# Storing output tiles of two batches with one transfer, and the order of the batches in the buffer for x

## The chip, the cores and the metric

The kernel runs on one core of a Trainium2 chip, as one launch. The metric is the device time of a launch in microseconds (us); all times below are in us unless ns is written. A launch works through five engines with instruction streams of their own: TensorE (PE in the profile, its weight loads PEld), VectorE (DVE), ScalarE (ACT), GpSimd (POOL) and SyncE (SP). SP does no arithmetic here, it issues transfers.

## What is computed

Blockwise causal attention, then a gated linear unit with a causal convolution over the sequence. Eight batches, eight heads, sequence 576, head width 64, model width 512:

```
scores = q @ k.T / 8, positions of later blocks of 64 masked
attn   = softmax(scores);  x = attn @ v        # x: 8 x 576 x 512, heads side by side
gate   = sigmoid(sum over 5 taps of conv_w[k] * x shifted by 4-k)
out    = (gate * (x @ w_val)) @ w_out          # float32, 8 x 576 x 512
```

## The kernel before

The work is cut into 32 pairs of heads, pair p being heads 2g and 2g+1 of batch b with b, g = divmod(p, 4). For each pair q and k are loaded, cast to fp16 and transposed, the scores go through the exponential on ScalarE, the product with v is normalised on VectorE (`norm`, L304) into a ring of four buffers x16, and the result is transposed into the buffer for x, `xts` (L149). The transpose goes one of two ways: through TensorE and a VectorE copy (`xtrans` L312, `evac_x` L326, words xtr and xt), or as a transposing transfer issued by SP (`xtrans_dma` L320, word xd).

`xts` holds 5 slots, each one batch of x: 128 partitions by 4 groups g by the sequence, with a few zero columns in front for the convolution. SLOT (L332) says which slot a batch takes. Eight batches share five slots, so the later ones write over earlier ones.

The second half goes by tiles. Tiles n = 0 to 7 are positions 0 to 511 of batch n. The last 64 positions of each batch are gathered: tile 8 has those of batches 0 to 3 (256 columns), tile 9 those of batches 4 to 7. ORDER (L333) gives the sequence 0, 1, 2, 3, 8, 4, 5, 6, 7, 9. `span` (L339) is the view of x that a tile reads: one slot for n below 8, and four neighbouring slots for tiles 8 and 9. For each tile there is a convolution on TensorE (`conv`, word cn), the tanh on ScalarE (`gate`, th), x @ w_val (`val`), the product of both on VectorE (`gated`, gv), and then for each block of 128 rows the product with w_out (`proj`, word o), its copy from PSUM to the output buffer `osb` by VectorE or ScalarE (`evac_out` L400, word oc) and a store (`store` L404, word st).

`osb` has NO = 5 buffers, given out in the order of TILES (L334), so an oc waits until the store five output tiles earlier has landed: (4,3) and (6,0) come after (8,0) and (4,3) in the same buffer, (5,0) after (8,1).

A block of 128 rows of tile 8 or 9 covers 64 positions of each of two batches. `store` writes these with two transfers of 64 partitions (loop at L409). Tile 8 has two blocks of 512 columns, (8,0) and (8,1). Tile 9 has (9,0) with 512 columns and its second block cut in two halves of 256 columns, (9,1) and (9,2). The last store of (9,2) is issued by ScalarE, all others of these by SP. In `xts` the batches 4 to 7 stand in falling order in slots 4 to 1, so the rows of tile 9 are those of batches 7, 6, 5, 4.

The order of all work is written out by hand: the string PLAN (L15) is a list of words that is run through from front to back, and each engine takes its own instructions in that order. The end of it, with the stores of tile 9:

```
o.7.4@3 gv.9.3 o.7.3@0 oc.7.4@A o.9.0@1 oc.7.3@D st.7.4 st.7.3 o.9.2@0 oc.9.0@A o.9.1@2 oc.9.2@D
st.9.0 oc.9.1@A st.9.2 st.9.1
```

After @ stand the PSUM banks, or the engine (A is ScalarE, D VectorE, P GpSimd). Waits between the engines, and between transfers and engines, follow from which data an instruction reads and writes. Transfers issued by SP and ScalarE share eight semaphores in rotation, and a transfer waits until the one eight before it has landed.

Of the kernel before, what the change touches and what calls it, by code (L numbers as in the profile page):

```python
# [90 lines left out]
def kernel(  # L91
# [10 lines left out]
    nc = tc.nc  # L102
# [5 lines left out]
    B, H, SEQ, D = q.shape  # L108
# [8 lines left out]
    X0 = 16  # L117
# [3 lines left out]
    def const(shape, dt, tag):  # L121
        return cpool.tile(shape, dt, tag=tag, name=tag)
# [26 lines left out]
    xts = const([128, 5, 4, X0 + SEQ + 64], fp16, "xt")  # L149
# [14 lines left out]
    def f16(i):  # L164
        return f32(i).bitcast(fp16)
# [154 lines left out]
    def xtrans_dma(p, m):  # L320
        b, g = divmod(p, 4)
        nc.sync.dma_start_transpose(
            out=xts[0:128, SLOT[b], g, X0:X0 + 640].rearrange("p (i t) -> p i t", t=128),
            in_=x16[p % NX16][0:128].rearrange("p i h d -> p (i h d)"))

    def evac_x(p, m):  # L326
        b, g = divmod(p, 4)
        nc.vector.tensor_copy(out=xts[0:128, SLOT[b], g, X0:X0 + SEQ],  # L328
                              in_=f16(bank["xtr", p])[:, 0:SEQ])


    SLOT = (0, 1, 2, 3, 4, 3, 2, 1)  # L332
    ORDER = (0, 1, 2, 3, 8, 4, 5, 6, 7, 9)  # L333
    TILES = [(n, t) for n in ORDER for t in range({7: 5, 8: 2, 9: 3}.get(n, 4))]  # L334

# [3 lines left out]
    def span(n, rows, g, back):  # L339
        if n < B:  # L340
            return xts[rows, SLOT[n], g, X0 - back:X0 - back + 512]
        return xts[rows, n - 8:n - 4, g, X0 + 512 - back:X0 + SEQ - back]

    def conv(n, *a):
        (*h, m), w = a, width(n)
        rows = [2 * h[0], 2 * h[0] + 1] if h else range(4)
        for row, b in zip(rows, m):
            bank["cn", n, row] = b
        for kk in range(5):
            for d in range(4):  # L350
                for row in rows:
                    g = (row + d) % 4
                    rs, cs = slice(32 * row, 32 * row + 32), slice(32 * g, 32 * g + 32)
                    mm(f32(bank["cn", n, row])[cs, 0:w], DG[rs, 5 * g + kk, 0:32], span(n, rs, g, 4 - kk),
                       start=(kk == 0), stop=(kk == 4))
# [20 lines left out]
    def val(n, x, m):  # L376
        bank["val", n, x] = m[0]
        for fc in range(4):
            mm(f32(m[0])[:, 0:width(n)], w_val_sb[0:128, fc, 128 * x:128 * x + 128],
               span(n, slice(0, 128), fc, 0), start=(fc == 0), stop=(fc == 3))  # L380
# [8 lines left out]
    def row(n, t):  # L389
        return min(t, {7: 3, 9: 1}.get(n, t))  # L390
# [13 lines left out]
    def store(n, t, m):  # L404
        c, o = cols(n, t), osb[0:128, TILES.index((n, t)) % NO]
        if n < B:
            (nc.scalar if t == 4 else nc.sync).dma_start(out=out[n, 128 * row(n, t):128 * row(n, t) + 128, c], in_=o[:, c])
            return
        for h in range(2):  # L409
            s = n - 8 + 2 * row(n, t) + h  # L410
            (nc.scalar if (n, t, h) == (9, 2, 1) else nc.sync).dma_start(
                out=out[s if n == 8 else 8 - s, 512:SEQ, c], in_=o[64 * h:64 * h + 64, c])

    def cols(n, t):
        z = t - {7: 3, 9: 1}.get(n, 9)
        return slice(256 * z, 256 * z + 256) if z >= 0 else slice(0, 512)
# [16 lines left out]
    def warm(m):  # L433
# [5 lines left out]
        "wv": scale_w_val, "wo": cast_w_out, "tq": trans, "Lqr": load_first, "cqr": cast_first, "tqr": trans_first, "kz": ends, "s": scores, "e": exps,  # L439
        "m": mask, "av": av, "n": norm, "xtr": xtrans, "xd": xtrans_dma, "xt": evac_x,  # L440
        "cn": conv, "th": gate, "val": val, "gv": gated, "o": proj, "oc": evac_out, "st": store,
        "cw": taps, "cT": evac_taps, "DG": diags, "w": warm, "Lcn": load_conv,
    }
# [58 lines left out]
```

## Time and profile before

| what | value |
|---|---|
| median of 3 runs | 171.03 (170.36 to 171.4) |
| time of the profiled execution | 171.92 |
| its span, first to last instruction | 170.1 |
| granted TensorE clock, mean | 0.981 |
| TensorE busy | 158.8 (93%) |
| VectorE busy | 127.8 (75%) |
| ScalarE busy | 125.7 (74%) |
| GpSimd busy | 98.8 (58%) |
| L411 stores on SP | 9, issued from 135.6 to 167.0 |
| L411 stores on ScalarE's queue | 1, issued at 164.9 |
| data written to HBM | 9.44 MB |

The profile is one execution, recorded by the hardware. Its times count from the first instruction. The page gives each engine's busy time, the chain of work that ended last, and groups of instructions by line; further views of the same trace list instructions in order of time (the timeline), transfers (the DMA view: packets, bytes, share of the 16 DMA engines, issues with the time to landing), and waits. A line of the timeline reads: start, busy time, engine and line, operation, output<-input, count, and in brackets the idle time before it with what ended it. SPq and ACTq are the instruction queues of SP and ScalarE: the issue of a transfer is shown there, not its flight. A transfer has landed when its semaphore has reached the full count.

### The profile page before, as it was taken

The numbers are of one execution on the slowest core, as the hardware profiler recorded it, in microseconds if no ns is written. First come the engines' busy times: TensorE is split into PE (matmuls) and PEld (weight loads), VectorE is DVE, ScalarE is ACT, GpSimd is POOL, SyncE is SP. The second block draws the span as 40 slices with busy tenths as digits, with TensorE's granted clock in tenths as the row PEclk, the third lists the DMA queues.
The fourth block names the chain that finished last, engine by engine and source line by source line (L and its number), as shares of the span: only waits on it lengthen the run. The fifth ranks groups of instructions, "written<-read, shape, count | busy, mean of one in ns | idle before, by whom it ended". The sixth has DMA issues, their size and how long they took to land.

```text
span 170.1 us, 7366 instructions
## 1 busy us (share of the span) xinstructions
PE 158.8 (93%) x3121; PEld 102.0 (60%) x3121; DVE 127.8 (75%) x271; ACT 125.7 (74%) x155; POOL 98.8 (58%) x190
## 2 busy tenths in 40 slices
PE   7769999999999999999989999999999999999970
PEld 2346877567675666587556766656756558454550
DVE  3884789879699989888986778766999459729540
ACT  5499999898886999789775897768787971440330
POOL 5279999996969469939760799265672362000000
PEclk9995999999999999999999999999999999999996
DMA  5999999999999605999798969993899899564554
GB/s 187 369 335 396 368 323 319 338 337 365 305 284 390 162 0 139 284 302 322 216 250 312 262 117 235 310 300 84 206 296 230 181 126 173 128 233 185 191 193 116
DMA packets 56027, 41.97 MB, mean 247 GB/s; under 512 B 46005, under 2 KB 46517, under 8 KB 55994
## 3 DMA queue, kind: packets, MB, share of 16 engines
q1 hardware_dynamic: 55770, 41.31, 85.3%
q8 instruction: 24, 0.39, 1.0%
q10 hardware_dynamic: 224, 0.20, 0.3%
q14 instruction: 9, 0.07, 0.1%
HBM read 30.42 MB, written 9.44 MB: 234 GB/s over the span
## 4 chain that ended last, share of the span: by engine, by line
PE 80%; ACT 5%; DMA 4%; DVE 3%; POOL 2%; issue 1%; SPq 1%; POOLq 0%; DVEq 0%
PE B L112 76%; ACT pt L278 5%; DMA qks<-in_q_dram 4%; PE B L315 3%; DVE x L308 1%; DVE xt L328 1%; SPq L174 1%; POOL qk L223 1%; DVE w_val L231 1%; DVE qT L239 0%; POOL v16t L220 0%; POOL v L217 0%; DVE rc L307 0%; POOL pt L286 0%; ACT osb L223 0%
## 5 line engine op out<-in xcount | busy, mean ns | idle before, releaser
L278 ACT ACTIVATE pt<-B 128x1024 f16<-128x1024 f32 x96 | 92.0, 1029 | 12.7 <-PE B L112 11.7
L223 POOL CAST qk<-qks 128x1152 f16<-128x1152 f32 (+2 forms) x31 | 41.3, 1343 | 10.4 <-DMA qks<-in_q_dram 5.5
L112 PEld LDWEIGHTS <-pt 128*128 128x128 f16 x960 | 34.2, 98 | 8.3 <-issue 1.9
L112 PE MATMUL B<-v,pt 128*128 128x65 f16 x896 | 36.4, 194 | 2.0 <-issue 1.0
L112 PE MATMUL B<-xt,w_val 128*128 128x512 f16 (+1 forms) x160 | 35.8, 359 | 0.4 <-DVE x L308 0.4
L112 PE MATMUL B<-w_out,gv 128*128 128x512 f16 (+1 forms) x152 | 36.2, 368 | 0.0
L112 PE MATMUL B<-qT,kT 32*128 32x448 f16 (+3 forms) x640 | 34.0, 292 | 2.1 <-DVE qT L239 1.1
L308 DVE TENSOR_TENSOR x<-B,rc 128x320 f16<-128x320 f32 x64 | 31.5, 492 | 2.4
L384 DVE SCALAR_TENSOR_TENSOR gv<-th,B 128x512 f16<-128x512 f32 (+1 forms) x40 | 24.5, 630 | 8.1 <-PE B L112 5.0
L372 ACT ACTIVATE th<-B 128x1024 f32<-128x1024 f32 (+1 forms) x20 | 17.7, 941 | 16.2 <-PE B L112 9.7
L112 PEld LDWEIGHTS <-kT 32*128 32x128 f16 x640 | 18.5, 93 | 16.4 <-issue 11.1
L112 PEld LDWEIGHTS <-w_val 128*128 128x128 f16 x160 | 14.0, 98 | 14.0 <-issue 2.1
L217 POOL CAST v<-vst 128x512 f16<-128x512 f32 x32 | 19.6, 618 | 4.0 <-PE B L112 1.7
L239 DVE STREAM_TRANSPOSE kT<-qk 128x576 f32<-128x576 f32 (+2 forms) x17 | 19.6, 1160 | 1.5 <-POOL qk L223 1.5
L112 PEld LDWEIGHTS <-gv 128*128 128x128 f16 x152 | 13.4, 98 | 11.0 <-issue 0.8
L239 DVE STREAM_TRANSPOSE qT<-qk 128x576 f32<-128x576 f32 (+3 forms) x18 | 19.4, 1103 | 0.4 <-POOL qk L223 0.3
L307 DVE RECIPROCAL rc<-B 128x5 f32<-128x5 f32 x64 | 11.8, 184 | 10.4 <-PE B L112 10.0
L286 POOL MEMSET pt<- 64x384 f16 x32 | 13.3, 414 | 9.8 <-ACT pt L278 8.1
L223 DVE COPY osb<-B 128x512 f32<-128x512 f32 (+1 forms) x21 | 13.7, 658 | 6.3 <-PE B L112 6.2
L285 POOL COPY pt<-pt 128x128 f16<-128x128 f16 x32 | 9.6, 301 | 13.2 <-ACT pt L278 12.8
L223 ACT COPY osb<-B 128x512 f32<-128x512 f32 (+1 forms) x17 | 9.5, 574 | 7.8 <-PE B L112 4.4
L112 PE MATMUL B<-xt,DG 32*32 32x512 f16 (+1 forms) x800 | 13.1, 356 | 0.0
(45 smaller groups left out, 112.6 us busy)
## 6 DMA issues: line engine op xcount, KB each, us to landing
qks<-in_k_dram SPq DMA_DIRECT2D x16, 576.0 KB, 6.3
qks<-in_q_dram SPq DMA_DIRECT2D x16, 576.0 KB, 6.8
vst<-in_v_dram SPq DMA_DIRECT2D x64, 128.0 KB, 5.4
out_dram<-osb SPq DMA_DIRECT2D x31, 256.0 KB, 3.1
vtst<-in_v_dram SPq DMA_DIRECT2D x8, 128.0 KB, 6.7
th<-in_moe_w_val_dram SPq DMA_DIRECT2D x2, 512.0 KB, 7.1
osb<-in_moe_w_out_dram SPq DMA_DIRECT2D x2, 512.0 KB, 5.7
out_dram<-osb SPq DMA_DIRECT2D x7, 128.0 KB, 2.4
```

The costliest lines, as they stand in the source:

```text
L112: nc.tensor.matmul(out=out, lhsT=lhsT, rhs=rhs, start=start, stop=stop, skip_group_check=True)
L217: nc.gpsimd.tensor_copy(out=v16s[p % NV][0:128, 0:4, 0:2, 0:64], in_=vst[p % NVS][0:128])
L223: (eng.copy if eng is nc.scalar else eng.tensor_copy)(out=o, in_=i)
L239: nc.vector.transpose(out=(qT, kT)[i][a % NQT][0:128].bitcast(fp32).rearrange("p c (x n) -> p c n x", n=9)[:, :, x // 2:y // 2], in_=qk16[ ...
L278: nc.scalar.activation(out=pts[(2 * a + r) % NPT][0:128, 0:2, 512 * t:512 * t + 512], in_=two(bank["s", a, t, 2 * r], bank["s", a, t, 2 * ...
L285: nc.gpsimd.tensor_copy(out=pt[0:128, 0:2, 1536:1600], in_=pt[0:128, 0:2, 0:64])
L286: nc.gpsimd.memset(pt[64:128, 0:2, 0:1536].rearrange("p h (t s) -> p h t s", t=3)[:, :, :, 0:64], 0.0)
L307: nc.vector.reciprocal(out=rc[0:128], in_=O[:, :, 64:65])
L308: nc.vector.tensor_tensor(out=x16[p % NX16][0:128, 0:5, h, 0:64], in0=O[:, :, 0:64], in1=rc[0:128].to_broadcast([128, 5, 64]), op=ALU.mult)
L315: nc.tensor.transpose(out=f16(m[0])[:, 128 * i:128 * i + 128], in_=x16[p % NX16][0:128, i, 0:2, 0:64], identity=ident16[0:128, 0:128])
L372: nc.scalar.activation(out=ths[ORDER.index(n) % NTH][0:128, 2 * r:2 * r + 2, 0:w], in_=two(bank["cn", n, 2 * r], bank["cn", n, 2 * r + 1], w),
L384: nc.vector.scalar_tensor_tensor(out=gvs[z % NG][0:128, x, 0:w], in0=ths[z % NTH][0:128, x, 0:w], scalar=1.0, in1=f32(bank["val", n, x])[: ...
```

## The change

The two transfers of a block of tile 8 or 9 become one of 128 partitions, whose output side is a view of three dimensions: 2 batches, 64 positions, the columns. For that the batches have to stand in rising order, so SLOT is given out anew and `span` reads tile 8 from slots 1 to 4 and tile 9 from slots 0 to 3. PLAN is unchanged; (9,2) is now issued by ScalarE as a whole.

```diff
-    SLOT = (0, 1, 2, 3, 4, 3, 2, 1)
+    SLOT = (1, 2, 3, 4, 0, 1, 2, 3)
...
-        return xts[rows, n - 8:n - 4, g, X0 + 512 - back:X0 + SEQ - back]
+        return xts[rows, SLOT[4 * n - 32]:SLOT[4 * n - 32] + 4, g, X0 + 512 - back:X0 + SEQ - back]
...
-        for h in range(2):
-            s = n - 8 + 2 * row(n, t) + h
-            (nc.scalar if (n, t, h) == (9, 2, 1) else nc.sync).dma_start(
-                out=out[s if n == 8 else 8 - s, 512:SEQ, c], in_=o[64 * h:64 * h + 64, c])
+        s = 4 * n - 32 + 2 * row(n, t)
+        (nc.scalar if (n, t) == (9, 2) else nc.sync).dma_start(
+            out=out[s:s + 2, 512:SEQ, c], in_=o[:, c])
```

In the changed kernel these stores stand in line 410.

## The prediction

> **What bounds the kernel now.** I read the page first (busy shares and the table of DMA issues), then the chain of work that ended last from 130 us on, then the timeline after 163.5 us, and last the DMA view and the timelines of VectorE and ScalarE in the stretches where the changed stores run.
>
> ```profile
> PE 158.8 (93%) x3121; PEld 102.0 (60%) x3121; DVE 127.8 (75%) x271; ACT 125.7 (74%) x155; POOL 98.8 (58%) x190
> ```
> ```profile
> 146.80 18.04 PE B L112 x248
> 164.83 0.02 issue
> 164.86 0.37 ACT osb L223
> ```
> ```profile
> 163.57 0.33 SPq L407 DMA_DIRECT2D out_dram<-osb  x1
> ...
> 164.59 3.04 SPq L411 DMA_DIRECT2D out_dram<-osb  x5
> ...
> 164.92 0.53 ACTq L411 DMA_DIRECT2D out_dram<-osb  x1
> ```
> TensorE is the bound: the chain is matmuls without a gap up to 164.83, then one ScalarE copy to 165.23. What is left of the span of 170.1 is the last stores. SP issues five of them one behind the other, 164.59 to 167.63 (about 0.6 each); by the trace's landing events the last one, issued at 167.05, lands at 169.11, and 0.99 of closing follows. So the end is set by SP's queue and by the landing of a store, and each store that lands later moves the end one for one.
>
> **The slots for x: nothing.** Batches 5, 6 and 7 went to slots 3, 2, 1 and go to 1, 2, 3. Tile 8 read slots 0 to 3 and reads 1 to 4. In both kernels the last reader of what batches 5 to 7 overwrite is tile 8's last value matmul (101.6 in the trace), on TensorE, which runs in order ahead of their first write. Batch 4 goes to slot 0 in place of the unused slot 4; its first write is issued at 94.09, and batch 0's last reading matmul ended at 55.1. The order on TensorE, VectorE, ScalarE and GpSimd is the same instruction by instruction, and so are their waits but for the numbers of the DMA semaphores. The cover is a wait that is over before it is asked for; were it gone, a store of x would wait for TensorE, and I see no place for that.
>
> **The stores: what is removed.** Ten stores of 64 partitions become five of 128. On SP four issues go (nine to five), on ScalarE's queue one stays one. Each L411 issue takes 0.48 to 0.60 us. In the middle (135.55 and 146.10) two issues of 0.6 go; there TensorE never waits for SP, so that is hidden. At the end SP would issue tile (9,0) at 164.59, and (9,1) when ScalarE's copy ends, 165.25, not at 166.45 and 167.05.
>
> **The stores: what is added.** The new transfer's output side is [2, 64, columns]: its outermost dimension is 2, with 128 rows of 2 KB (or 1 KB) behind it. Its SBUF side is 128 partitions. No transfer of this kind is in the trace. What the trace says on how a transfer is shared out: of 162 transfers, 161 raise their semaphore by 16 separate landings, and all have 64 or 128 as outermost dimension on both sides. One does not, the load of the 5x512 conv weights, the only one in the table of DMA issues without a time to landing:
> ```profile
> conv_nat<-in_moe_conv_w_dram SPq DMA_DIRECT2D x1, 10.0 KB
> ```
> Its semaphore gets one event at 3.19, 0.58 us after the issue, when no data can have come, and five between 8.44 and 9.57. So an outermost dimension of 5 was worked by 5 DMA engines, not 16. An outermost dimension of 2 on one side can then be shared fairly by 2; if the SBUF side decided alone it would be 16. I take 2: the same split has to hold for both sides.
>
> The Trainium skill (DMA: Bandwidth & Descriptors, Why a DMA increments its semaphore by 16 and not by 1) states the rule behind that row: the number of engines is the largest one up to 16 that divides the slowest dimension of both sides, and the sequencer adds the rest of the 16 at once. By that rule it is 2 here, on the lowest-numbered engines each time; the trace agrees for the 5-row load, and no run here shows two unequal sides.
>
> What one engine carries:
> ```profile
> DMA packets 159, 0.29 MB, mean 293 GB/s; under 512 B 16, under 2 KB 16, under 8 KB 159
> ...
> q1 hardware_dynamic: 159, 0.29, 77.5%
> ```
> ```profile
> DMA packets 288, 0.26 MB, mean 219 GB/s; under 512 B 32, under 2 KB 288, under 8 KB 288
> ...
> q10 hardware_dynamic: 144, 0.13, 32.9%
> q1 hardware_dynamic: 144, 0.13, 32.3%
> ```
> The first is 160.9 to 161.9, stores of whole 2 KB rows: 77.5% of 16 engines over 1.0 us is 12.4 us for 143 rows, 86 ns a row. The second is 163.8 to 165.0, two stores of 1 KB rows: 65.2% of 16 x 1.2 us for 256 rows, 48 ns. With 2 engines each gets 64 rows: 5.5 us for a store of 2 KB rows, 3.1 us for one of 1 KB rows.
>
> **At the end.** (9,0) is issued at 164.59, first packet 1.0 later as now, 165.6. (9,1) and (9,2) are queued on the same two engines behind or among it: 5.5 + 3.1 + 3.1 = 11.7, so 177.3, and 0.35 from the last packet to the landing (as now): 177.6 against 169.11, **+8.5**. Bounds: +8.2 if the first packet comes as soon as for a 128-row store (0.85, and a little less to the landing); +11 if 1 KB rows take 67 ns each as in the 64-row stores now (59 to 75 in the trace), 64 x 2 x 67 = 8.6 in place of 6.2.
>
> **In the middle, tile (8,0).** Its store is issued at 135.55; the engines come to it at 136.8; 5.5 us later, 142.3, it is read out and lands about 142.7. Now it lands at 140.37. VectorE's copy of tile (4,3) takes the same buffer (five rotate) and waits for it:
> ```profile
> 140.23 0.49 DVE L308 TENSOR_TENSOR x<-B,rc 128x320 f16<-128x320 f32 x1
> 140.64 0.68 DVE L223 COPY osb<-B 128x512 f32<-128x512 f32 x1
> 141.24 0.18 DVE L307 RECIPROCAL rc<-B 128x5 f32<-128x5 f32 x1
> ...
> 142.71 0.49 DVE L308 TENSOR_TENSOR x<-B,rc 128x320 f16<-128x320 f32 x1
> ```
> VectorE is busy without a gap from there to 145.1, and the multiplication that ends at 143.20 gives conv 6 its PSUM bank, which starts at 143.33. So the copy at 142.75 in place of 140.64 moves TensorE by **2.1**. The x transposes queue behind the same rows: that of pair 27 then lands near 143.7, not 140.98, and n.31.0 (141.45 now) waits for it: 2.2. The two overlap; I take 2.2. Bounds: 1.5 (rows begin earlier) and 3.5, if the instruction fetch of 16 KB that took 1.17 us at 138.2 falls on one of the two engines.
>
> **In the middle, tile (8,1).** Issued at 146.10 (+2.2, less up to 1.0 since SP was held up 2.16 us by the transpose before it), 5.5 us of rows, landing at 152.2 to 153.05 on the old clock, not 149.17. Waiting for its buffer is the copy of (5,0):
> ```profile
> 149.26 0.69 DVE L223 COPY osb<-B 128x512 f32<-128x512 f32 x1
> 152.98 0.69 DVE L223 COPY osb<-B 128x512 f32<-128x512 f32 x1 [3.02 <-PE B L112]
> ```
> That copy frees PSUM bank 2 for value tile 9.2, which starts at 151.48: TensorE waits 1.4 to 2.3, say **1.9**. The copy of (6,0) at 152.98 needs the store of (4,3), which now stands behind (8,1) on the two engines: 1.4 to 2.4, the same stretch. From there VectorE is busy to 158.05, so nothing gives it back.
>
> **Sum.** 2.2 + 1.9 + 8.5 = 12.6. On the profiled execution: span 170.1 to 182.7, its time of 171.92 to 184.5. That execution is 0.9 above the median of 171.03, on which I put the difference: **183.6**. The forecast's own range is 171.03 + (1.5 + 1.4 + 8.2) to 171.03 + (3.5 + 2.4 + 11): 182.1 to 187.9.
>
> **Rivals.**
> *All 16 engines (the change pays).* It decides if the SBUF side's 128 sets the split. Then (9,1), issued at 165.25, lands by the 1.72 of a 128-row store of 1 KB rows now at 166.97, or at 167.7 by the 2.43 of the slowest 64-row store: 2.1 to 1.4 less than 169.11. The middle is hidden. Time 171.03 - 2.0 = 169.0. For it: all wide stores land in 16 parts. Against: the 5-row load. The Trainium skill (DMA: Bandwidth & Descriptors, Rules for kernel authors) speaks for it too, advising one 128-partition transfer over two of disjoint halves; the 64-row stores' landing of 2.0 to 2.4 against 1.7 to 2.0 agrees, but the rule leaves the outermost dimension open.
>
> *Two engines, the middle hidden.* VectorE and the buffers would have to take 2.3 us each time; the copies at 140.64 and 149.26 start 0.1 to 0.3 after the landing they wait for, which speaks against it. 171.03 + 8.5 = 179.5.
>
> *Two engines, another pair each time.* Then the end is (9,0) alone: 165.6 + 5.5 + 0.35 = 171.5, +2.4. With the middle: 171.03 + 4.1 + 2.4 = 177.5. No row tells which engines the 5-row load used.
>
> *Two engines and SP held up.* If SP cannot queue more behind two full engines (issues of 1.56 and 2.16 us at 138.2 and 143.9 show it held), the transposes of x come later still and TensorE waits beyond 3.5: over 188.
>
> **How the numbers follow.** Forecast 0.59, middle hidden 0.14, another pair 0.06, held up 0.08, all 16 engines 0.13. The time is the likeliest case's, 183.6. The range of 177.0 to 188.5 takes in the first three cases (0.79) and a part of the fourth. About 1% (1.7 us) is what a measurement of this kernel can tell from no change: the 16-engine case, a gain of 1.4 to 2.1, is split 0.09 faster and 0.04 the same; all others are slower, 0.87.
>
> **What would show it.** In the profile after: the five L410 stores land 5 us or more after the issue (7 to 13 at the end), the DMA share after 165 is about 2 engines of 16 (0.13) for over 10 us, and SP's closing wait for the output grows from 1.4 to about 12. VectorE's copies of (4,3) and (5,0) begin with an idle stretch ended by a DMA, and TensorE shows two gaps of about 2 us, before conv 6 and value 9.2. Stores that land in about 2 us would make the forecast wrong at its first step, and the time would be near 169.

## The result and the profile after

| | before | after |
|---|---|---|
| median | 170.88 (4 runs) | 186.12 (186.01 to 186.41, 4 runs) |
| ratio | | 1.0894, interval 1.0858 to 1.0931 |
| span of the profiled execution | 170.1 | 184.2 |

The change makes the kernel slower by 15.2. The forecast was 183.6 in a range of 177.0 to 188.5.

Two distances within one execution carry the comparison, because the executions differ by a microsecond or two in their first 100 us: from the issue of the store of (8,0) to that of (9,0), which is the middle, and from the issue of (9,0) to the last landing, which is the end. Issues are from the timeline, landings from the trace's semaphore events.

| | (8,0) to conv 6 | (8,0) to (8,1) | (8,0) to (9,0): middle | (9,0) to last landing: end |
|---|---|---|---|---|
| before | 7.78 | 10.55 | 29.04 | 4.52 |
| after | 11.27 | 14.45 | 35.95 | 13.49 |

The middle has grown by 6.9 and the end by 9.0, 15.9 together. The spans differ by 14.1 because the profiled execution of before issued its store of (8,0) at 135.55 and that of after at 133.75, 1.8 sooner; that stretch is the same work in both (the kernel with the slots alone, below, has it at 134.24).

**How many engines.** The end of the changed kernel, first the timeline from 169 us, then the DMA view from 179.2 to 182.8, when only the two transfers of 1 KB rows are left:

```profile
169.70 1.17 SPq L410 DMA_DIRECT2D out_dram<-osb  x2
169.96 0.37 ACT L223 COPY osb<-B 128x256 f32<-128x256 f32 x1 [0.29 <-PE B L112]
170.02 1.10 ACTq L410 DMA_DIRECT2D out_dram<-osb  x1
```
```profile
q1 hardware_dynamic: 121, 0.12, 9.7%
q10 hardware_dynamic: 51, 0.05, 3.9%
```
All issues end by 171.2, sooner after the last copy than before (0.8 after it, not 2.4). But SP's and ScalarE's transfers together then keep 13.6% of 16 engines busy, the work of 2.2 engines. The semaphores say the same: each of the five merged stores has three events, one about 1 us after the issue and two at the end ((9,0): 170.66, 179.26, 179.27), where a store of 64 rows had 16. The three stores of tile 9 land at 179.27, 181.66 and 183.19, one behind the other, as they would on the same two engines. The stores issued behind that of (8,1) show the two engines directly: of the first of them, issued at 148.86, 14 of its 16 parts have landed by 152.44 and the last two at 156.19 and 156.44, after (8,1). What it costs at the end stands in SP's waits for stores, here before (from 160 us on) and after (from 164 us on):

```profile
SPq L497 <- DMA out_dram<-osb: 1.4, 1, 1.4
```
```profile
SPq L496 <- DMA out_dram<-osb: 12.3, 2, 10.8
```

**The middle.** The chain of waits from 125 us on, which before was matmuls from end to end (pieces, start and length):

```profile
124.93 9.58 PE B L112 x158
134.52 9.23 DMA xt<-x
...
143.84 0.49 DVE x L308
...
147.48 0.66 SPq L322
148.14 0.05 issue
148.20 7.63 DMA out_dram<-osb
155.82 0.02 issue
155.84 0.70 DVE osb L223
156.55 0.04 issue
156.59 13.35 PE B L112 x152
```
It runs through two transfers now: the x transpose of pair 27, issued behind the store of (8,0) and landing after 9.23, and the store of (8,1), landing after 7.63. Between them lie VectorE's normalisations, which that transpose holds up, and the issues of the transposes that follow from these. From value tile 9.2 at 156.59 on it is matmuls again, 152 of them in 13.35.

The timeline of the same stretch shows each wait with what ended it (the bracket):

```profile
141.56 0.69 DVE L223 COPY osb<-B 128x512 f32<-128x512 f32 x1 [2.60 <-DMA out_dram<-osb]
...
142.30 0.59 PE L112 MATMUL B<-v,pt 128*128 128x65 f16 x14 [2.04 <-DVE osb L223]
...
143.84 0.49 DVE L308 TENSOR_TENSOR x<-B,rc 128x320 f16<-128x320 f32 x1 [1.49 <-DMA xt<-x]
...
145.02 2.98 PE L112 MATMUL B<-xt,DG 32*32 32x512 f16 x80 [0.72 <-DVE x L308]
...
155.84 0.69 DVE L223 COPY osb<-B 128x512 f32<-128x512 f32 x1 [1.85 <-DMA out_dram<-osb]
156.59 0.60 PE L112 MATMUL B<-xt,w_val 128*128 128x256 f16 x4 [0.21 <-DVE osb L223]
```
VectorE's copy of (4,3) waits for the store of (8,0), and its copy of (5,0) for that of (8,1). There is one thing more: conv 6 takes 2.98 for its 80 matmuls, where it took 1.35 before. The line from the timeline of before:

```profile
143.33 1.35 PE L112 MATMUL B<-xt,DG 32*32 32x512 f16 x80
```

The stretches of the profile after show why. Each row gives the stretch, its length, the busy time of PE, PEld, DVE, ACT and POOL with the number of instructions, the granted clock, the DMA share and GB/s:

```profile
138.00:144.00 6.00, 3.77 (x95) 3.10 (x91) 1.88 (x6) 0.13 (x1) 1.59 (x6) 1.00 1.04 106
144.00:151.00 7.00, 6.17 (x89) 2.68 (x90) 3.99 (x12) 2.52 (x3) 0.00 (x0) 0.51 0.58 109
151.00:157.00 6.00, 5.79 (x107) 3.04 (x105) 3.03 (x5) 1.94 (x2) 0.00 (x0) 1.00 0.53 139
```
After TensorE had idled, its granted clock was 0.5 from 144.0 to 150.9. From conv 6 to conv 7 it needs 8.18 in place of 5.12.

The transpose of pair 27 is later than the store of (8,0) alone makes it. That store has landed at 141.54, and 15 of the transpose's 16 parts land from 142.09 to 142.24, but the last one at 143.75. Between them lies one packet of 16 KB of the instruction queue, 141.52 to 142.67, in the DMA view from 141.4 to 142.7:

```profile
q8 instruction: 1, 0.02, 5.5%
```
It begins as the rows of (8,0) end. That it held the engine of the last part fits these times, but the record does not name a packet's engine, so it is not shown.

### The profile page after: what moved, and what is told of

It is laid out like the page before. It is cut to its first block, busy times and chain, and to the rows that moved or that the text cites. A ratio compares the mean times of both kernels' runs of the same rounds, so it can differ in the third digit from the quotient of the medians.

```text
span 184.2 us, 7357 instructions
## 1 busy us (share of the span) xinstructions
PE 160.8 (87%) x3121; PEld 102.0 (55%) x3121; DVE 127.7 (69%) x271; ACT 125.6 (68%) x155; POOL 98.8 (54%) x190
## 4 chain that ended last, share of the span: by engine, by line
PE 64%; DMA 11%; ACT 9%; DVE 6%; issue 1%; SPq 0%; DVEq 0%
PE B L112 61%; ACT pt L278 9%; DMA xt<-x 5%; DMA out_dram<-osb 4%; PE B L315 3%; DMA qks<-in_k_dram 2%; DVE x L308 2%; DVE qT L239 1%; DVE xt L328 1%; DVE rc L307 1%; DVE w_val L231 1%; DVE kT L239 0%; DVE osb L223 0%; SPq L322 0%; DVE qk L223 0%
## 5 line engine op out<-in xcount | busy, mean ns | idle before, releaser
L112 PE MATMUL B<-xt,w_val 128*128 128x512 f16 (+1 forms) x160 | 37.4, 369 | 0.6 <-DVE x L308 0.4
L112 PE MATMUL B<-xt,DG 32*32 32x512 f16 (+1 forms) x800 | 14.7, 381 | 0.8 <-DVE x L308 0.7
```

Of the source, the lines that this page charges most:

```text
L112: nc.tensor.matmul(out=out, lhsT=lhsT, rhs=rhs, start=start, stop=stop, skip_group_check=True)
```

## The experiments

The theory: the merged store runs on as many DMA engines as its outermost output dimension, two; late landings of (8,0) and (8,1) hold VectorE and TensorE in the middle, and three such stores on the same two engines end the kernel. Rivals: the slots; the form of the transfer (three dimensions, rows of two batches) rather than the outermost dimension; a middle that is hidden; a halved clock that is a cost of its own or none.

**1. The slots alone.**
```diff
-        s = 4 * n - 32 + 2 * row(n, t)
-        (nc.scalar if (n, t) == (9, 2) else nc.sync).dma_start(
-            out=out[s:s + 2, 512:SEQ, c], in_=o[:, c])
+        for h in range(2):
+            s = 4 * n - 32 + 2 * row(n, t) + h
+            (nc.scalar if (n, t, h) == (9, 2, 1) else nc.sync).dma_start(
+                out=out[s, 512:SEQ, c], in_=o[64 * h:64 * h + 64, c])
```


> The new SLOT and span as in the change, but each block of tiles 8 and 9 stored by two transfers of 64 partitions again. Theory (the merged store runs on two DMA engines, because the outermost dimension of its output side is 2): the slots cost nothing, so 170.9, within 1% of before; stores of tiles 8 and 9 land 2.0 to 2.4 after their issue at the end; TensorE has no gap before conv 6. Rival (the new slots make x wait or move the loads): slower by a part of the 15 that the change costs, over 172.6, with waits on the writes of x.

Measured 171.3 against 171.43 for before on the same chip: ratio 1.000, interval 0.997 to 1.003. Middle 29.15, end 4.52, as before. The slots cost nothing.

**2. Three dimensions again, with position outermost.** The gated product of tiles 8 and 9 is written in another order, so that a block is 32 positions of four batches:
```diff
+        if n >= B:
+            o, i, v = o.rearrange("p (s b) -> p b s", b=4), *(y.rearrange("p (b s) -> p b s", b=4) for y in (i, v))
...
-            out=out[s:s + 2, 512:SEQ, c], in_=o[:, c])
+            out=out[s:s + 4, x:x + 32, c].rearrange("b s c -> s b c"), in_=o[:, c])
```


> One transfer of 128 partitions per block as in the change, and again three dimensions on the output side, but position outermost: [32 positions, 4 batches, columns]. For that the gated product of tiles 8 and 9 is written in the order position, batch; nothing is left out. Theory (outermost dimension decides): 32 and 128 share 16, so 16 engines and 16 landings, 1.7 to 2.4 from issue to landing, the last store issued about 0.4 after the one of tile (9,0): 169.0, between 168.4 and 170.2, faster than before by 1%. Rival (a transfer with three dimensions, or with rows of two batches, is slow in itself): about 186 as the changed kernel.

Measured 169.84 against 171.43, ratio 0.9908, interval 0.9873 to 0.9942: 0.9% faster than before, a small gain but clear of no change, and far below the changed kernel. Its DMA view from 164.8 to 166.5 has the three stores of tile 9 in flight:

```profile
q1 hardware_dynamic: 257, 0.38, 62.0%
q10 hardware_dynamic: 144, 0.13, 23.1%
```
Here 85% of 16 engines are at work, in a transfer that has three dimensions as in the change and goes to four batches. So neither the form nor the number of batches makes the store slow; the outermost dimension does. Middle 28.97, end 3.15 (4.52 before): the merged stores save 1.4 at the end once they run on 16 engines, and each lands after 2.4 to 2.5.

**3. Merged store for tile 8 alone**, and **4. for tile 9 alone**, where the condition is n == 9.
```diff
+        if n == 8:
+            s = 4 * n - 32 + 2 * row(n, t)
+            (nc.scalar if (n, t) == (9, 2) else nc.sync).dma_start(
+                out=out[s:s + 2, 512:SEQ, c], in_=o[:, c])
+            return
+        for h in range(2):
+            s = 4 * n - 32 + 2 * row(n, t) + h
...
```


> Merged store (outermost dimension 2) for tile 8 alone, two transfers per block for tile 9. Theory: the end is as before (last landing 4.5 after the first store of tile 9 is issued, not 13.5), and the middle costs what the trace of the changed kernel shows: 3.5 up to the start of conv 6, 3.1 of halved clock behind it and 0.4 at value tile 9.2, so 177 to 178. Rival (the middle is hidden and all of the cost is at the end): 171. Rival (the halved clock has nothing to do with the stores): 174 to 175.

> Merged store for tile 9 alone, two transfers per block for tile 8. Theory: the middle is as before, and the end costs 9.0 (13.5 in place of 4.5 from the issue of the first store of tile 9 to the last landing): 179.9, between 179 and 181. Rival (the end is late only because the middle had filled the queue): near 171.

Experiment 3 measured 177.95 (ratio 1.0397, interval 1.0353 to 1.0440) with a middle of 36.35 and an end of 4.54. Experiment 4 measured 179.9 (1.0514, interval 1.0471 to 1.0556) with a middle of 29.14 and an end of 13.54. The parts are independent: 4.0% and 5.1% add up to 9.1%, where the change has 8.9%, within the intervals. The rival of a hidden middle is out, and so is that of an end that is late only through what the middle left in the queue. The 177 to 178 expected of experiment 3 came out, but by luck in part: the sum had the halved clock in it, and experiment 5 shows that this term was wrong.

**5. TensorE kept busy in the gaps.** The changed kernel with matmuls on zeros (word w) in the plan (the twelve and the four words are written short here):
```diff
-av.29.0@1 av.29.1@3 n.31.1 av.30.0@4 n.29.0 xd.31 av.30.1@5 n.29.1 cn.6@0167
+av.29.0@1 w@4 (12 times) av.29.1@3 n.31.1 av.30.0@4 n.29.0 xd.31 w@5 (4 times) av.30.1@5 n.29.1 cn.6@0167
```


> The changed kernel with 16 matmuls on zeros (0.21 each) put into the plan where TensorE stood idle in it: 12 ahead of the product of pair 29 (idle of 2.04), 4 ahead of the second product of pair 30 (idle of 0.25 and 0.72 behind it). Work is added, none left out. Theory (conv 6 starts late through VectorE and the landing of tile (8,0) and of the x transpose; the idle stretch in addition halves the granted TensorE clock for 6.83 behind it, which costs 3.1): conv 6 starts as late as in the changed kernel (11.3 after the issue of store (8,0)), but no stretch at 0.5 follows, so 183.0, between 182.5 and 183.8. Rival (the halved clock comes from somewhere else, or the matmuls behind conv 6 are slow because the transfers hold them up): 186 or more, with the stretch at 0.5 still there.

Measured 187.84 against 170.54, ratio 1.0976, interval 1.0906 to 1.1047: a miss, it is not faster than the changed kernel (whose interval its own overlaps). The rival does not fit either, for the stretch at 0.5 behind conv 6 is gone. The timeline of TensorE:

```profile
140.38 2.75 PE L112 MATMUL B<-wz 128*128 128x512 f16 x12
...
145.29 1.72 PE L112 MATMUL B<-xt,DG 32*32 32x512 f16 x80
...
156.67 0.84 PE L112 MATMUL B<-xt,w_val 128*128 128x256 f16 x4 [2.71 <-DVE osb L223]
```
The clock stays up as expected (conv 6 in 1.72, from conv 6 to conv 7 5.49, granted clock 1.00 from 138 to 156.8), conv 7 starts at 150.78 and not at 153.20. And value tile 9.2 starts at 156.67, where it started at 156.59. The last pieces of the chain of waits say why:

```profile
148.32 7.59 DMA out_dram<-osb
155.91 0.02 issue
155.93 0.70 DVE osb L223
156.63 0.04 issue
156.67 15.03 PE B L112 x152
```
The store of (8,1) is issued by SP, behind x transposes that wait for VectorE and not for TensorE's clock: at 148.32 here and at 148.20 in the changed kernel, and it lands 7.6 later in both. In the changed kernel the 3.1 of slow matmuls lay in the shadow of that landing, that is, TensorE would have had to wait for it anyway. My theory that they cost 3.1 falls. Here TensorE, done sooner, idles 2.71 ahead of value 9.2, and the clock is 0.50 from 156.9 to 160.3, with nothing beside it: the same 152 matmuls take 15.03 in place of 13.35. That 1.7 is a cost of the halved clock where TensorE is last.

**6. Outermost dimension 4.** Four batches by 32 positions, every second one:
```diff
+            w = g[:, fc, i:i + 128] if n < B else g[:, fc, i // 128:256:2]
...
-            out=out[s:s + 2, 512:SEQ, c], in_=o[:, c])
+            out=out[s:s + 4, x:SEQ:2, c], in_=o[:, c])
```


> One transfer per block, output side [4 batches, 32 positions, columns], every second position: outermost dimension 4. For that the product with w_out reads every second column of the gated product; nothing is left out. Theory (as many engines as the outermost dimension): 4 engines, five semaphore events per store (one at once, four landings), 32 rows of 86 or 46 ns per engine, so 2.8 less for the store of tile (8,0) and 5.8 less at the end than with 2: last landing 7.5 to 8.5 after the issue of (9,0), no halved clock or less of it: 174.5 to 177. Rival (two-part split whatever the outermost dimension, as soon as a transfer has three dimensions with a batch outside): 186. Rival (16 engines once four batches are there): 170.

Measured 178.1 against 170.54, ratio 1.0469, interval 1.0374 to 1.0565. Each store has five semaphore events ((9,0): 166.94, 171.56, 171.67, 172.16, 172.19), and the DMA view from 172 to 174 shows twice what the changed kernel has at that point, 27.2% or 4.4 engines:

```profile
q1 hardware_dynamic: 92, 0.09, 13.8%
q10 hardware_dynamic: 93, 0.10, 13.4%
```
So it is four engines; the time lies above the range of the theory and far from both rivals. Middle 31.36 (+2.3), end 8.96 (+4.4), no halved clock there. The time is 1.1 above what I expected, and the end 0.5 above: the rows of an engine make 5.7 of it, but from the first packet to the last it is 7.4. The first 1.8 us of the store of (9,0) see only 21 rows, where four engines at 84 ns would do 86.

| | (8,0) to conv 6 | (8,0) to (8,1) | middle | end |
|---|---|---|---|---|
| slots alone | 7.89 | 10.39 | 29.15 | 4.52 |
| position outermost (16 engines) | 7.71 | 10.09 | 28.97 | 3.15 |
| four batches outermost (4) | 9.07 | 10.93 | 31.36 | 8.96 |
| merged tile 8 alone (2) | 11.49 | 14.83 | 36.35 | 4.54 |
| merged tile 9 alone (2) | 7.88 | 10.58 | 29.14 | 13.54 |
| TensorE kept busy (2) | 11.70 | 14.73 | 37.88 | 13.48 |

## Why the prediction was right

**The slots: nothing.** Right, 1.000 in experiment 1. One reading on the way was not: batch 0 stands in slot 1 of the changed kernel, and slot 0 is unused until batch 4 takes it, as slot 4 was before. So the first write of batch 4 has no reader to wait for at all.

**Two engines.** Right. The row it was taken from, the load of five rows, has 5 on both sides; that the smaller of two unequal sides decides was an assumption, which the runs now bear out. The Trainium skill (DMA: Bandwidth & Descriptors, Rules for kernel authors) says that an outermost dimension below 16 confines a transfer to at most that many engines. The trace agrees with it for two and four, and with the page's common divisor of both sides (Why a DMA increments its semaphore by 16 and not by 1) for 2 against 128, 4 against 128 and 32 against 128. The rule in favour of the change, one transfer of 128 partitions in place of two of 64, held here only where the outermost dimension was large enough: it paid with 32 in experiment 2, and not with 2 or 4.

**The end, +8.5.** Measured 9.0. The rows went at 84 and 46 ns, 11.3 per engine where I had 11.7. What was missing is a slow start: from the first packet to the last it is 12.0, and the first packet came 1.18 after the issue, not 1.0. Same engines each time: right, and the rival with another pair per store falls.

**The middle, 2.2 + 1.9 = 4.1.** The mechanism was right, and the waits are those named (the copies of (4,3) and (5,0), the transpose of pair 27, value 9.2); the term was mis-sized, it is 6.9. To conv 6 it is 3.5, the upper bound, and from there to (9,0) 3.4, above the bound of 2.4. Three things made it so. The store of (8,0) landed 7.8 after its issue, where I had 7.1, and that of (8,1) after 7.6, where I had about 7: the slow start again. The transpose of pair 27 landed 2.2 after the store of (8,0), where I had 1.0, with a packet of 16 KB of the instruction queue beside it; if that held one of the two engines, it is the case for which the prediction had set its upper bound of 3.5. And I let (8,1) be issued 1.2 to 2.2 later; it was 3.9, for the transposes ahead of it on SP wait for VectorE's normalisations, which the late transpose of pair 27 holds up in turn. The rival "SP held up" has its share in this: the two transposes at 137.19 and 139.17 took 1.88 and 2.44 to issue, but the time stayed below 188.

One sign did not come. The prediction has a gap of about 2 ahead of value 9.2; TensorE's gap there is 0.21, because the slow matmuls fill it. With the clock kept up, in experiment 5, it is 2.71.

**The sum.** 12.6 forecast, 15.2 measured between the medians, 15.9 by the two distances. By these the middle was 2.8 short and the end 0.5. The median of 186.12 is 2.5 above the forecast of 183.6 and inside the range that the prediction adds up from its terms, 182.1 to 187.9. The halved clock was not foreseen; that this did the forecast no harm is luck, for by experiment 5 it cost nothing in the changed kernel.

**The 16-engine rival.** It did not come about in the change, but experiment 2 is what it described, and the gain of 1.6 there (0.9% of 171.43) lies in the 1.4 to 2.1 worked out for it.

Left open is why a transfer on few engines starts slowly: no run here separates the making of its 64 rows per engine from their fetching. That (8,0) and (8,1) might be stored later or to other buffers was not tried, since the version with position outermost removes the cause.

## What to carry to other kernels

Before two transfers are made one, look at the outermost dimension of both sides of the new pattern: two blocks of DRAM with a gap put a 2 there, and the transfer crawls on two of 16 engines (256 KB landed after 7.6 to 9.6 here, where the same blocks on 16 engines, in experiment 2, took 2.4 to 3.2). If the rows can be put in another order further up, so that a dimension over which all 16 engines share stands outermost, such as the 32 positions of experiment 2, the merged transfer can pay. And a slow store is not hidden because nobody reads it: whoever takes its buffer next waits, and transfers that are issued behind it on the same engines wait with it.

## What the runs showed that I had not expected

The granted TensorE clock fell to 0.5 after idle stretches of 2 to 3 us. In the changed kernel an idle of 2.04 within 140.3 to 142.3 was followed by 0.5 from 144.0 for 6.83; in experiment 5 an idle of 2.71 by 0.50 from 156.9 for 3.41; with tile 8 alone merged, an idle of 2.23 from 140.5 on by 0.5 from 144.3 for 6.83. The Trainium skill (TensorE: Matmul & The Clock Gate, Why this matters for your kernels) warns of idle gaps above about 3 us; in these three rows the fall followed 2.0 to 2.7. That the idle alone decides is not shown: in the last of these runs an idle of 1.98 from 5.9 on was not followed by any fall.

Stores on two or four engines moved little in their first 2 us: after the first packet of (9,0) at 170.88 there are 24 rows in 2.2 us, where two engines at 84 ns do 52. The store of (9,0) on 16 engines in experiment 2 shows no such stretch: 89 rows in its first 0.5 us, where 16 engines at 84 ns do 95.
